# A third chunk of the dense layers beside the last rounds of an attention kernel

## The chip, the core and the metric

The kernel runs on one core of a Trainium2 chip. The core has five engines that run side by side, each with its own list of instructions in a fixed order: TensorE (PE, matrix products; PEld is its loading of weights), VectorE (DVE), ScalarE (ACT), GpSimd (POOL) and SyncE (SP, which here issues all transfers between memory and the core). An instruction waits until semaphores say that its inputs are there and its output's place is free; everything behind it on its engine waits with it. The metric is the time of one execution in microseconds (us) on the device, as the median of several runs.

## The reference

Three layers follow each other. x has 4 batches of 768 tokens and 512 columns.

```
attention: per head (8 heads, width 64) and per chunk of 32 tokens: softmax over 8 memory keys
           and the keys from 16 before to 8 behind the chunk, times the values
moe:       4 experts of width 64: causal softmax attention over 768 tokens, output wo[e],
           weighted by the gate (the best 2 of 4 experts for each token)
mixer:     h = transpose(x) @ U @ V          (U 768 x 32, V 32 x 768: mixes tokens)
           u = x + transpose(h)
           out = u + relu(u @ w_ch1) @ w_ch2 (w_ch1 512 x 2048, w_ch2 2048 x 512)
```

Below, "the attention" is all up to u, and "the dense layers" are the last line.

## The kernel before

Every product is made of three in a reduced precision (high part times high part, low times high, high times low), so each matrix is split into a high part (a copy on ACT) and a low part (a subtraction on DVE).

**The dense layers by chunks of tokens.** The 3072 tokens are taken in NCH = 6 chunks of 512. u is not formed: the kernel keeps z, which has 256 columns (the experts' outputs before wo, mixed), and multiplies w_ch1 by wo beforehand (`fuse_w1`, for four blocks j of 512 of the 2048 hidden columns; weights `wp_h`, `wp_l`). The 2048 hidden columns are 16 blocks f of 128. They are done in two parts:

- *Blocks f = 0 to 3 (FA = 4)*, in the plain way. For each chunk c, `load_z` loads z and splits it (`zh` on ACT, `zl` on DVE); `gemm1` makes one block of hidden columns: six matmuls `ph` (L285) of 512 columns, then `hh` (ACT, L293) and `hl` (DVE, L294); `gemm2` multiplies it by w_ch2: 3 matmuls `po` (L301) for each f and each of 4 output blocks m; `save_part` copies each finished `po` to `o` and stores it (L306, L308, L309). A chunk is 24 `ph` and 48 `po`, 72 matmuls of 512 columns in all.
- *Blocks f = 4 to 15* and the residual, by the scheme with seven products of half blocks (`right`, `multiply`, matmuls `acc`, L934). `right` makes the hidden block `t` (ACT, L866), sums of its quarters `sx` (DVE, L873), and splits them to `xhi` (ACT, L876) and `xlo` (DVE, L877). This is the last stage; it takes the chunks 0 to 5 again, one after the other.

**Three stretches.** (1) The attention, in rounds; the last batch (b = 3) has 12. Beside its rounds 0 to 5 block j = 0 of `fuse_w1` and the w_ch2 weights of the first part are prepared, and then `early` does the first part for the chunks below NEC. `early` is a generator: `fill` and `take` write its steps between and behind the rounds; each engine's order is then made when the program is built, by the readiness of steps and with the attention's steps ahead of `early`'s. (2) When the attention's pools are closed, `late` does the first part for the chunks NEC to 5; a second generator, `bg`, runs beside it and prepares the weights of the last stage: `fuse_w1` for j = 1, 2, 3 (matmuls `w1p`, L249) and `load_pair` for the pairs of blocks 8, 10, 16, 12, 14. The weights come as 64-bit numbers, and `decode` turns each block of 256 columns into 32 bit: a transfer `raw` (L122), one ACT step (L126), and three steps on DVE (L127, L128, L129); the split follows (L134 and L135, or L190 to L193). These transfers go to a pool that takes the place of the attention's buffers, so the first one waits until the attention's last result has been stored: that is `z` (DVE, L657, from matmuls `pz`, L656), stored as `zs` (L658). (3) The last stage. Its buffers (`hp`) are opened after `bg` has made its pairs up to 10 (`ready`).

```python
        late = list(range(NEC, NCH))
...
                if nxt is None and f == FS:
                    while not ready():
                        next(bg)
                    pass_a.close()
                    hp = p2.enter_context(tc.tile_pool(name="hp", bufs=1, side="right"))
...
                    for _ in range(BGA if nxt else 2 * BGA):
                        if not ready():
                            next(bg)
```

Of the kernel before, what the change touches and what calls it, by code (L numbers as in the profile page):

```python
# [52 lines left out]
VMP = 2  # L53
MS = 2
FA = 4
NEC = 2
BGA = 3
ND0, NW0, ND1, NW1 = 2, 2, 6, 3
LATE = 12
# [33 lines left out]
def tile_chunk_attention__moe_attention__mixer(  # L93
# [169 lines left out]
    def load_z(c):  # L263
        zf = (zp if wp2 is None else ea).tile([128, 2, CT], F32, name="zf", bufs=NZF)
        o = 0
        while o < CT:
            b, t = divmod(c * CT + o, S)
            n = min(CT - o, S - t)
            nc.sync.dma_start(zf[:, :, o:o + n], zs[b][:, :, t:t + n])
            o += n  # L270
        zh = zp.tile([128, 2, CT], F32R, name="zh", bufs=NZ)
        zl = zf.bitcast(F32R) if wp2 is None else zp.tile([128, 2, CT], F32R, name="zl", tag="zf", bufs=NZ)
        nc.scalar.copy(zh, zf)  # L273
        nc.vector.tensor_sub(zl, zf, f32(zh))
        zhl[c] = zh, zl
        zfs[c] = zf
# [34 lines left out]
    def early(ps):  # L311

        for c in range(NEC):
            load_z(c)
# [516 lines left out]
    with ExitStack() as p2:  # L831
# [49 lines left out]

        late = list(range(NEC, NCH))
        load_z(late[0])
# [170 lines left out]
```

## Time and profile before

| | us |
|---|---|
| median of 3 runs | 863.04 |
| the 3 runs | 862.87, 863.04, 864.9 |
| the profiled execution | 859.0 |
| its span, from the first to the last instruction | 857.2 |
| PE busy in the span | 811.0 |
| DVE busy in the span | 630.5 |
| ACT busy in the span | 494.8 |

In the profiled execution the attention's last product `pz` stands at 450.35 us, the first `acc` matmul of the last stage at 536.87 us. Between them lies the second stretch. Matmuls are pipelined: one of 512 columns is shown as about 0.39 us long, but the next one starts about 0.23 us after it. A busy share of PE is therefore no measure of how much of its time it used.

### The profile page before, as it was taken

How to read it: one execution, taken by the hardware profiler on the slowest of the kernel's cores; microseconds unless marked ns; L12 is line 12 of the kernel's file. 1: busy time of each engine (PE TensorE's matmuls, PEld its weight loads, DVE VectorE, ACT ScalarE, POOL GpSimd, SP SyncE). 2: the span in 40 equal slices, each digit the busy share in tenths (PEclk: the TensorE clock that was granted, in tenths of full speed). 3: DMA queues.
4: the chain of work that ended last, by engine and by line, in shares of the span. 5: the costliest groups of instructions: out<-in, count | busy, mean ns of one | idle time of the engine just before them, and what ended most of it. 6: DMA issues, size and time to landing. Idle time of an engine off the chain costs nothing.

```text
span 857.2 us, 18057 instructions
## 1 busy us (share of the span) xinstructions
PE 811.0 (95%) x6404; PEld 727.1 (85%) x6404; DVE 630.5 (74%) x1997; ACT 494.8 (58%) x1464; POOL 168.0 (20%) x254
## 2 busy tenths in 40 slices
PE   7889999999999998889979999999999999999995
PEld 5778999889987897768767878999989989899995
DVE  5687766577767766899536899989578495775947
ACT  3587766577656755656434566656464454645533
POOL 5334343344433424222110000000000000000002
PEclk8799999999999999999999999999999999999999
DMA  9644422133222201253206744301203012030101
GB/s 246 181 122 112 111 76 75 57 98 107 50 68 76 85 1 45 86 182 108 74 19 200 226 159 148 99 25 50 75 1 123 1 50 75 1 124 1 62 38 50
DMA packets 59627, 74.74 MB, mean 87 GB/s; under 512 B 29456, under 2 KB 34064, under 8 KB 58768
## 3 DMA queue, kind: packets, MB, share of 16 engines
q1 hardware_dynamic: 59536, 73.57, 27.9%
q8 instruction: 51, 0.84, 0.4%
q14 instruction: 40, 0.33, 0.1%
HBM read 57.83 MB, written 15.73 MB: 86 GB/s over the span
## 4 chain that ended last, share of the span: by engine, by line
PE 72%; DVE 9%; DMA 8%; ACT 6%; issue 3%; SPq 1%; POOL 1%; DVEq 0%; ACTq 0%; POOLq 0%
PE acc L934 23%; PE ph L285 14%; PE t L665 7%; PE pqk L468 5%; DMA raw<-in_w 4%; PE pv L508 3%; PE s L417 3%; PE tpc L600 3%; PE po L301 3%; PE sc L548 3%; PE sc L549 2%; PE tp L437 2%; DMA part<-o 2%; ACT a L424 1%; ACT ac L560 1%
## 5 line engine op out<-in xcount | busy, mean ns | idle before, releaser
L934 PE MATMUL acc<-xhi,sw 128*128 128x256 f32 x1008 | 191.6, 283 | 0.9 <-ACT xhi L876 0.9
L934 PEld LDWEIGHTS acc<-xhi,sw 128*128 128x128 f32 x1008 | 160.6, 189 | 8.1 <-ACT xhi L876 2.2
L934 PE MATMUL acc<-xlo,sw 128*128 128x256 f32 x504 | 139.2, 283 | 0.0
L873 DVE TENSOR_TENSOR sx<-t 128x256 f32<-128x256 f32 x180 | 67.8, 420 | 72.0 <-ACT t L866 72.0
L866 ACT ACTIVATE t<-ph 128x512 f32<-128x512 f32 x72 | 43.0, 597 | 121.2 <-PE ph L285 121.2
L582 POOL TENSOR_SCALAR ac<-ac,su,g 128x128 f32<-128x128 f32 (+5 forms) x96 | 70.0, 738 | 157.7 <-DVE su L580 102.7
L934 PEld LDWEIGHTS acc<-xlo,sw 128*128 128x128 f32 x504 | 95.4, 189 | 2.6
L925 POOL TENSOR_TENSOR pt<-pt,cp 128x512 f32<-128x512 f32 x3 | 6.4, 2155 | 408.6 <-DVE xlo L877 408.6
L876 ACT CAST xhi<-sx 128x256 fp32r<-128x256 f32 x210 | 76.0, 407 | 13.8 <-PE acc L934 6.2
L424 ACT ACTIVATE a<-a,nm 128x96 f32<-128x96 f32 x192 | 69.9, 367 | 22.9 <-DVE nm L421 22.2
L877 DVE TENSOR_TENSOR xlo<-sx,xhi 128x256 fp32r<-128x256 f32 x210 | 80.1, 421 | 3.8 <-ACT xhi L876 3.3
L560 ACT ACTIVATE ac<-sc,nmc 128x128 f32<-128x128 f32 (+5 forms) x96 | 60.4, 632 | 35.3 <-DVE nmc L575 20.3
L285 PE MATMUL ph<-zh,wp_l 128*128 128x512 f32 x192 | 61.0, 398 | 1.0 <-ACT zh L273 1.0
L417 PE MATMUL s<-k_t,qbd 128*128 128x96 f32 x384 | 56.3, 284 | 5.3 <-DMA k_t<-in_kw 4.0
L600 PE MATMUL tpc<-ident_s,ac 128*128 128x128 f32 x336 | 54.0, 279 | 7.0 <-ACT ath L603 2.9
L285 PE MATMUL ph<-zh,wp_h 128*128 128x512 f32 x192 | 60.3, 394 | 0.0
L429 POOL TENSOR_TENSOR a<-a,rs 128x288 f32<-128x288 f32 x64 | 42.6, 668 | 82.1 <-DVE rs L428 23.2
L417 PEld LDWEIGHTS s<-k_t,qbd 128*128 128x128 f32 x384 | 51.2, 200 | 8.1 <-issue 4.0
L285 PE MATMUL ph<-zl,wp_h 128*128 128x512 f32 x176 | 56.6, 393 | 0.0
L548 PE MATMUL sc<-kl,qs 128*128 128x384 f32 (+2 forms) x144 | 51.3, 357 | 2.6 <-DVE z L657 1.4
L421 DVE CUSTOM_DVE_ANT_0 a<-s,band_s 128x96 f32<-128x96 f32 x192 | 40.2, 252 | 16.6 <-PE s L417 13.9
L600 PEld LDWEIGHTS tpc<-ident_s,ac 128*128 128x128 f32 x336 | 39.5, 143 | 13.0 <-issue 6.2
(174 smaller groups left out, 2038.7 us busy)
## 6 DMA issues: line engine op xcount, KB each, us to landing
raw<-in_w SPq DMA_DIRECT2D x64, 256.0 KB, 3.5
k_t<-in_kw SPq DMA_DIRECT2D x32, 288.0 KB, 3.4
v_t<-in_vw SPq DMA_DIRECT2D x32, 288.0 KB, 3.2
qbd<-in_qT SPq DMA_DIRECT2D x64, 96.0 KB, 2.8
part<-o SPq DMA_DIRECT2D x24, 256.0 KB, 2.5
pt<-part SPq DMA_DIRECT2D x6, 1024.0 KB, 4.9
out<-pt SPq DMA_DIRECT2D x24, 256.0 KB, 2.5
zf<-zs SPq DMA_DIRECT2D x8, 512.0 KB, 4.7
```

Source lines behind the costliest of these rows:

```text
L285: nc.tensor.matmul(p, w[f // 4][:, pr, fs], z[:, pr], start=(n == 0), stop=(n == 5))
L417: nc.tensor.matmul(s[:, j, :], w["q"][:, qd * 3 + j], w["k"][:, qd * 3 + j], start=True, stop=True)
L424: nc.scalar.activation(a[:, j, :], a[:, j, :], AF.Exp, bias=nm[:, j:j + 1], scale=-1.0, accum_out=ss[:, j:j + 1])
L548: nc.tensor.matmul(s[:, o:o + w], q, kl[b, e, hf][:, :w], start=True, stop=False)
L560: nc.scalar.activation(aa[h][:, :n], src, AF.Exp, bias=nm[:, h:h + 1], scale=1.0, accum_out=su[:, h:h + 1])
L582: nc.gpsimd.tensor_scalar(aa[h][:, :n], aa[h][:, :n], su[:, h:h + 1], gates[b, i // 3][:, i % 3, 2 * pr + h:2 * pr + h + 1], op0=ALU.mult, ...
L600: nc.tensor.transpose(tp[h][:, j * 128:(j + 1) * 128], aa[h][:, j * 128:(j + 1) * 128], ident_s)
L665: session.append(nc.tensor.matmul(*a, **kw).ins)
L873: nc.vector.tensor_tensor(x, t[:, p[0], p[1]], t[:, q[0], q[1]], op=op)
L876: nc.scalar.copy(hi, x)
L877: nc.vector.tensor_sub(lo, x, f32(hi))
L934: nc.tensor.matmul(acc[n][:, m], w[:, ms], x, start=(f == FA and u == 0 and m == 0), stop=(f == NF - 2 and u == 2 and m == 1))
```

## The change

The number of chunks that `early` takes goes from two to three. The number that `late` takes falls from four to three. No operation is added or removed.

```diff
-NEC = 2
+NEC = 3
```

What each engine is given when the program is built changes as follows. First PE, at the end of the attention (`sc`: scores, `tpc`: transposes of the scaled exponentials `ac`, `t`: their product with the values, `pyt`: transposes for the mixer). Before, from a round's scores on:

```order
L549 MATMUL sc<-kd,qs 128x256
L551 LDWEIGHTS identb_s
L551 MATMUL sc<-tri_s,identb_s 128x128
L600 MATMUL tpc<-ident_s,ac 128x128 x8
L628 MATMUL pyt<-ident_s,yT 128x128 x6
L665 MATMUL t<-ath,vt 64x128 x8
```

Now, at the same place:

```order
L600 MATMUL tpc<-ident_s,ac 128x128 x4
L285 MATMUL ph<-zh,wp_l_5577 128x512 x2
L285 MATMUL ph<-zf,wp_h_5576 128x512 x2
L285 MATMUL ph<-zh,wp_h_5576 128x512 x2
L301 MATMUL po<-hh,w2l_5599 128x512
L285 MATMUL ph<-zh,wp_l_5577 128x512 x2
L285 MATMUL ph<-zf,wp_h_5576 128x512 x2
L285 MATMUL ph<-zh,wp_h_5576 128x512 x2
L301 MATMUL po<-hl,w2h_5598 128x512
L301 MATMUL po<-hh,w2h_5598 128x512
L600 MATMUL tpc<-ident_s,ac 128x128 x4
L628 MATMUL pyt<-ident_s,yT 128x128 x6
```

The third early chunk's `ph` and `po` stand between the transposes: 15 matmuls here, then 21 behind `pyt`, 18 behind the next round's scores, 6 between the two halves of the following transposes and 12 behind them, of which the last six are the first `ph` of the first late chunk. In all 72 more matmuls of 512 columns stand ahead of the last `pz` than before; from there to the first `acc` there are 72 fewer.

Second, DVE, from the attention's last `z` on. Before:

```order
L294 SCALAR_TENSOR_TENSOR hl<-ph,hh 128x512
L657 TENSOR_TENSOR z<-pz,yT 128x768
L274 TENSOR_TENSOR zl<-zf,zh 128x1024
L127 TENSOR_SCALAR d_t<-d_t 128x256
L128 SCALAR_TENSOR_TENSOR d_t<-raw_6567,d_t 128x256
```

Now:

```order
L294 SCALAR_TENSOR_TENSOR hl<-ph,hh 128x512
L657 TENSOR_TENSOR z<-pz,yT 128x768
L127 TENSOR_SCALAR d_t<-d_t 128x256
L128 SCALAR_TENSOR_TENSOR d_t<-raw_6680,d_t 128x256
L127 TENSOR_SCALAR d_t<-d_t 128x256
```

In both the decoding of `bg`'s weights follows at once. From the first of these L127 up to the first `xlo` of the last stage DVE has 184 instructions before and 187 now. Of the kinds, four `hl` fewer, and one L127, one L128, one L190 and four `sx` more; all others are as many as before.

Third, DVE at the start of the last stage. Before:

```order
L193 TENSOR_TENSOR swrh<-sw_7608,swrh 128x256
L193 TENSOR_TENSOR swrh<-sw_7612,swrh 128x256
L127 TENSOR_SCALAR hd_7906<-hd_7906 128x256
L873 TENSOR_TENSOR sx<-t 128x256
L190 TENSOR_TENSOR sw_7620<-hd_7601 128x256
L877 TENSOR_TENSOR xlo<-t,xhi 128x256
```

Now:

```order
L127 TENSOR_SCALAR hd_7905<-hd_7905 128x256
L873 TENSOR_TENSOR sx<-t 128x256
L190 TENSOR_TENSOR sw_7619<-hd_7600 128x256
L190 TENSOR_TENSOR sw_7623<-hd_7600 128x256
L873 TENSOR_TENSOR sx<-t 128x256 x4
L128 SCALAR_TENSOR_TENSOR hd_7905<-raw_7918,hd_7905 128x256
L127 TENSOR_SCALAR hd_7905<-hd_7905 128x256
L877 TENSOR_TENSOR xlo<-t,xhi 128x256
```

Four sums `sx` come ahead of the first `xlo`. On SP the order around the attention's last store stays: the last `zs` store, then six `raw` loads; the four stores of the third chunk's result now stand ahead of the `zs` stores.

## Rows read from the trace of the kernel before

**Rows 1.** Windows: us, busy PE, PEld, DVE, ACT, POOL; clock, DMA share, GB/s.
```profile
422.52:450.35 27.83, 21.94 (x187) 17.22 (x186) 11.15 (x22) 9.76 (x22) 3.67 (x4) 0.94 0.06 24
450.35:460.15 9.80, 8.81 (x38) 7.10 (x39) 2.69 (x3) 1.96 (x3) 0.00 (x0) 1.00 0.42 131
460.15:534.38 74.23, 72.31 (x382) 61.37 (x381) 68.14 (x187) 44.37 (x107) 0.00 (x0) 1.00 0.59 194
534.38:600.00 65.62, 65.62 (x456) 61.08 (x455) 61.95 (x172) 41.33 (x110) 0.00 (x0) 1.00 0.17 57
```

**Rows 2.** Timeline of PE at the attention's end: start, duration, [idle before <-releaser].
```profile
422.52 1.53 PE L665 MATMUL t<-ath,vt 128*64 128x128 f32 x24
...
426.13 0.63 PE L600 MATMUL tpc<-ident_s,ac 128*128 128x128 f32 x4 [0.77 <-ACT ath L603]
426.82 0.87 PE L628 MATMUL pyt<-ident_s,yT 128*128 128x128 f32 x6
...
431.93 1.62 PE L600 MATMUL tpc<-ident_s,ac 128*128 128x128 f32 x10 [1.40 <-ACT ac L560]
434.56 1.31 PE L665 MATMUL t<-ath,vt 128*64 128x128 f32 x20 [1.01 <-DVE ath L603]
...
438.22 0.59 PE L656 MATMUL pz<-v_st,qm 96*128 96x384 f32 x2 [1.57 <-DVE qm L648]
438.65 0.82 PE L600 MATMUL tpc<-ident_s,ac 128*128 128x128 f32 x6
440.02 1.33 PE L600 MATMUL tpc<-ident_s,ac 128*128 128x128 f32 x6 [0.55 <-DVE z L657]
441.15 1.27 PE L628 MATMUL pyt<-ident_s,yT 128*128 128x128 f32 x5
442.41 2.12 PE L665 MATMUL t<-ath,vt 128*64 128x128 f32 x24
444.89 0.33 PE L628 MATMUL pyt<-ident_s,yT 128*128 128x128 f32 x1 [0.37 <-ACT yT L618]
...
450.35 0.62 PE L656 MATMUL pz<-v_st,qm 96*128 96x384 f32 x2
```

**Rows 3.** The same timeline; 35 more matmuls of 512 columns stand between these two.
```profile
452.98 0.39 PE L301 MATMUL po<-hh,w2l 128*128 128x512 f32 x1
...
461.16 0.62 PE L285 MATMUL ph<-zl,wp_h 128*128 128x512 f32 x2
```

**Rows 4.** Windows as in rows 1, around the fall of the clock.
```profile
430.00:440.00 10.00, 5.34 (x54) 3.98 (x53) 4.47 (x9) 3.71 (x9) 1.94 (x2) 1.00 0.01 2
440.00:444.00 4.00, 3.98 (x29) 3.62 (x31) 0.96 (x1) 0.36 (x1) 0.00 (x0) 0.57 0.25 98
```

**Rows 5.** The chain that ended last, in order of time: start, us, what.
```profile
451.61 0.96 DVE z L657
...
452.58 4.29 DMA zs<-z
...
457.87 4.60 DMA raw<-in_w
```

**Rows 6.** Timeline of DVE: the first decoding step and the first `xlo`.
```profile
460.15 0.29 DVE L127 TENSOR_SCALAR d_t<-d_t 128x256 uint32<-128x256 uint32 x1 [6.46 <-ACT d_t L126]
...
534.38 0.42 DVE L877 TENSOR_TENSOR xlo<-t,xhi 128x256 fp32r<-128x256 f32 x1
```

**Rows 7.** Timeline of PE: the first matmuls of the last stage.
```profile
536.87 0.40 PE L934 MATMUL acc<-xhi,sw 128*128 128x256 f32 x2
```

**Rows 8.** Waits of DVE from 460.15 to 534.4: total us, times, longest.
```profile
DVE d_t L127 <- ACT d_t L126: 8.2, 4, 6.5
DVE o L308 <- DMA part<-o: 2.8, 2, 2.2
```

**Rows 9.** DVE's work in that stretch by line: busy us, mean ns of one.
```profile
L294 DVE SCALAR_TENSOR_TENSOR hl<-ph,hh 128x512 fp32r<-128x512 f32 x12 | 8.2, 684 | 0.3 <-ACT hh L293 0.3
...
L873 DVE TENSOR_TENSOR sx<-t 128x256 f32<-128x256 f32 x1 | 0.4, 419 | 0.0
```

## The prediction

> **What bounds the kernel now.** I read the busy time by windows first, since the whole span hides that the stretches have different limits. In the last stage PE is busy without a gap, 65.62 of 65.62 us from 534.38 on [rows 1]; nothing there changes, so whatever moves the first `acc` moves the end by the same amount. The question is when that first matmul, now at 536.87 [rows 7], can start. Two stretches lie before it.
>
> At the attention's end, from 422.52 to the last `pz` at 450.35, PE is busy 21.94 of 27.83 us [rows 1]. The timeline shows why: short products that wait for each other's copies. The reader is to see the idle times in brackets, 0.77, 1.40, 1.01, 1.57, 0.55 and 0.37, together 5.67 us [rows 2], which a product that depends on none of this could fill. There is a second loss. The granted clock is 1.00 up to 440 and 0.57 from 440 to 444, that is mostly the lower level of 1.2 GHz, after ten microseconds in which PE was busy for 5.34 [rows 4]. The same 24 `t` matmuls take 1.53 us at 422.52 and 2.12 at 442.41 [rows 2].
>
> Between `pz` and `acc` PE seems full too, 72.31 of 74.23 us. But DVE is busy 68.14 of the same 74.23 [rows 1], nearly all of it `bg`'s weights. So two engines are close to full in this stretch, and the change takes work from only one of them.
>
> **The change, term by term**, against the profiled execution's 859.0 us.
>
> *1. Seventy-two matmuls come ahead of `pz`.* From 452.98 to 461.16 36 matmuls start, one every 0.227 us [rows 3]. 72 x 0.227 = **+16.4 us** on PE's list before the attention's last product. The list is in order, so an attention matmul that is ready stands behind them.
>
> *2. The idle time that they fill.* They stand behind the first half of the `tpc` at 425, behind the scores before 431.93, and around the `tpc` before 434.56. That covers the waits of 0.77, 1.40 and 1.01 us, **-3.2 us**. The groups there are 15, 18 and 12 matmuls, 3.4, 4.1 and 2.7 us, longer than the waits, so the rest is pure delay; the 21 behind `pyt` stand where PE did not wait at all. The waits of 1.57, 0.55 and 0.37 lie in the last chain of `pz`, `tpc` and `pyt`, where no new matmul is put. Bounds: nothing is filled (if ACT and DVE, which get the chunk's copies too, answer later by as much), or all 5.67.
>
> *3. The clock.* If PE is kept busy from 430 to 440, the clock should not fall. At full clock the 24 `t` would take 1.53 for 2.12, the six `tpc` 0.82 for 1.33, the five `pyt` about 0.8 for 1.27 (from six at 0.87) [rows 2]: 0.6 + 0.5 + 0.5 = **-1.6 us**. Bounds 0 and -1.6. The Trainium skill, TensorE: Matmul & The Clock Gate (Part 1), says that the array's clock is halved by default and that activity releases it; by that, too, the 1.6 us are given back, and [rows 4] agree as far as they show a fall behind a thinly used stretch.
>
> So the last `pz` moves by 16.4 - 3.2 - 1.6 = **+11.6 us**, to about 462 (bounds +9.1 and +16.4).
>
> *4. From `pz` to the decoding.* `z` is made at 451.61, its store takes 4.29 us to land, the first `raw` loads follow [rows 5], and DVE, idle for 6.46 us, starts decoding at 460.15 [rows 6]. The loads need the place of the attention's buffers, so they can't start sooner: these 9.80 us [rows 1] stay behind `pz` and move with it. The third chunk's four stores stand ahead of `zs` on SP, but its last `po` stand ahead of the last but one `pz` already, so I cost them at nothing; were they late, a store's landing, 4.29 us in [rows 5], would be about what they add.
>
> *5. DVE's work up to the first `xlo`.* Its list has four `hl` fewer, at 0.684 us [rows 9] 2.7 us; and more: one L127 at 0.29 [rows 6], one L128, one L190 and four `sx`, all of 128x256, at 0.419 like the `sx` in [rows 9], 0.29 + 6 x 0.419 = 2.8 us. The sum is **0.0**: DVE still has 68.1 us of work [rows 1]. The other side is PE: its 86.5 us from `pz` to `acc` fall by 16.4 to 70.1, while DVE's way is 9.8 + 68.1 = 77.9 without a single gap. PE arrives early and waits; what was taken from it is not gained.
>
> *6. DVE's gaps.* Of the 74.23 us it was idle 6.1. The largest causes are the landing of the first loads (8.2, of which 6.46 are those ahead of 460.15) and `o`'s two buffers, 2.8, waiting for stores [rows 8]. Both loads and stores keep their pattern; four fewer `hl` mean a little less waiting on ACT. I take **-1.0 us**, with -6.1 (no gap left) and +4 (one more wait for a store's landing of some 4 us) as bounds.
>
> *7. From the first `xlo` to `acc`.* Now 2.5 us pass (534.38 to 536.87) because PE comes later than DVE. With PE waiting instead, the first `acc` can follow at once: **-2.2 us**, bounds 0 and -2.5. Afterwards DVE, 61.95 of 65.62 us busy from there to 600 [rows 1], has as much to do as before, and the sums that four `sx` made early are missing later; I cost this at nothing. If PE's head start is spent waiting for `xlo` instead, this term is 0.
>
> Sum: 11.6 + 0.0 - 1.0 - 2.2 = **+8.4 us**, 867.4 against 859.0. The profiled execution stands 4.0 us below the median of the runs, 863.04; with that the forecast is **871.4 us**, slower by 1.0%. All bounds together give +0.5 (9.1 - 6.1 - 2.5) and +20.4 (16.4 + 4).
>
> **The rivals.**
>
> *PE stays the bound, and the change gains.* Then the 72 matmuls are only moved, and the filled waits and the clock are the result: -3.2 - 1.6 = -4.8, or 858.2 us. For it: PE's 72.31 of 74.23 busy [rows 1], and the idle brackets [rows 2], which are real. It decides only if DVE gets from `pz` to `acc` in about 70 us; term 5 gives 77.9 as the least. But a busy share of PE counts overlapping matmuls (0.39 us each, one every 0.227), while DVE's counts work. The Trainium skill, Perfetto Trace Analysis (Optimization Strategy), says that where the busiest engine changes over time, interleaving such regimes may improve a kernel; that is this rival, and the rows show the interleaving on PE but not on DVE, whose work stays where it was. Chance 6%.
>
> *Everything falls well: no change.* All idle time is filled, DVE loses nearly all gaps, `acc` follows at once: +0.5 to +2.6, 863.5 to 865.6 us. For it: gaps on DVE do shrink when PE runs ahead. Against it: most have their cause in transfers. Chance 13%.
>
> *Nothing is absorbed.* ACT and DVE get 4 `hh`, 4 `hl`, a split of z and four copies more in the attention's end, in order, between the steps that the chain waits for; if each wait only moves, terms 2 and 3 fall away (+4.8), and if the clock falls while PE waits in the second stretch, and is low where `acc` begins, some 2 us more are lost, as from 440 to 444: about 878 us. For it: PE will wait there some 12 us in all. Against it: DVE is busy 11.15 of 27.83 us at the attention's end [rows 1]. Chance 12%.
>
> *The chunk is not put where the change means it.* The new order shows it between the rounds, so this is out.
>
> **How the numbers follow.** 69% for the forecast, 6%, 13% and 12% for the others. Its own bounds reach from about +4 to +13 (term 2 or 3 missing, or gaps half gone). The range leaves out the gain and the best of the no-change cases below, and the far end of the last rival above: 865.0 to 878.0. A difference of 0.3%, 2.6 us, is about what a measurement of this kernel can tell from none: 6% faster, 13% within, 81% slower.
>
> **What would show it.** Right: the last `pz` 10 to 13 us later, with the waits before `tpc` and `t` gone and no fall of the clock there; the first decoding step about 10 us behind `pz`; DVE's busy time between that and the first `xlo` again near 68 us; and new waits of PE in that stretch, some 10 us, on `w_l` and `w_h` of `fuse_w1` and on `xhi` or `xlo`, where before there were 2 us. Wrong: a `pz` that moves by under 8 us; or a DVE that starts or ends this work sooner, above all loads that begin before the last `zs` store has landed; or a first `acc` less than 80 us behind `pz`.

## The result, and the profile after

The changed kernel takes 872.2 us (median of 4 runs, 870.62 to 874.0), the kernel before 863.17 us on the same chip. The ratio is 1.0101 with a 95% interval of 1.0077 to 1.0125: slower by 1.0%, +9.0 us, where +8.4 us was forecast.

The profiled execution of the changed kernel has a span of 870.7 us and a time of 872.46 us, about its median; that of the kernel before was 4.0 us below its own. So the two traces differ by 13.5 us, 4.5 more than the medians. Part of it can be seen: the `t` of 24 at the head of the attention's end starts at 424.71 in place of 422.52 [rows 2], 2.2 us before any of the 72 matmuls in question. The rest is therefore read in steps from that row on.

The first view is the table of windows of the changed kernel (us, then busy time of PE, PEld, DVE, ACT, POOL; granted clock, DMA share, GB/s), cut at the same events as [rows 1].

```profile
424.71:463.75 39.04, 36.04 (x259) 28.95 (x258) 16.43 (x29) 14.08 (x29) 3.69 (x4) 1.00 0.15 53
463.75:471.59 7.84, 6.19 (x20) 4.75 (x21) 1.56 (x3) 1.03 (x2) 0.00 (x0) 0.78 0.38 128
471.59:548.22 76.63, 65.37 (x339) 55.71 (x338) 68.44 (x190) 45.04 (x111) 0.00 (x0) 0.93 0.59 188
548.22:614.00 65.78, 65.48 (x450) 61.05 (x449) 59.14 (x166) 38.59 (x100) 0.00 (x0) 0.98 0.13 41
```

In the first line stand 259 matmuls where there were 187, and the stretch is 39.04 us long in place of 27.83. In the third PE is busy 6.9 us less than before, but DVE has 68.44 us of work for 68.14, and the stretch did not become shorter: 76.63 for 74.23. That is the change in two lines: 11 us are paid ahead of `pz`, and almost nothing comes back behind it.

| Step | before | after | difference | forecast |
|---|---|---|---|---|
| `t` at the attention's end to the last `pz` | 27.83 | 39.04 | +11.2 | +11.6 |
| last `pz` to the first decoding step of DVE | 9.80 | 7.84 | -2.0 | 0 |
| first decoding to the first `xlo` | 74.23 | 76.63 | +2.4 | -1.0 |
| first `xlo` to the first `acc` | 2.49 | -0.15 | -2.6 | -2.2 |
| first `acc` to the end of the span | 320.33 | 322.63 | +2.3 | 0 |
| sum | | | +11.3 | +8.4 |

The sum is 2.3 us more than the medians differ by. Which step is too long in these two executions cannot be told from them.

The timeline of PE at the attention's end in the changed kernel answers to [rows 2].

```profile
452.68 0.59 PE L656 MATMUL pz<-v_st,qm 96*128 96x384 f32 x2 [1.57 <-DVE qm L648]
453.11 0.82 PE L600 MATMUL tpc<-ident_s,ac 128*128 128x128 f32 x6
454.49 0.85 PE L600 MATMUL tpc<-ident_s,ac 128*128 128x128 f32 x6 [0.55 <-DVE z L657]
455.17 0.71 PE L628 MATMUL pyt<-ident_s,yT 128*128 128x128 f32 x5
456.38 1.53 PE L665 MATMUL t<-ath,vt 128*64 128x128 f32 x24 [0.51 <-DVE ath L603]
458.28 0.33 PE L628 MATMUL pyt<-ident_s,yT 128*128 128x128 f32 x1 [0.37 <-ACT yT L618]
...
463.75 0.44 PE L656 MATMUL pz<-v_st,qm 96*128 96x384 f32 x1
```

The waits of 1.57, 0.55 and 0.37 us are still there, as they were forecast to be; those of 0.77, 1.40 and 1.01 are gone from this stretch, and one of 0.51 is new. The second `tpc` takes 0.85 us where it took 1.33, the 24 `t` 1.53 where they took 2.12 [rows 2].

The windows of the changed kernel show the granted clock, first at the place of [rows 4], then where the last stage begins.

```profile
430.00:440.00 10.00, 10.00 (x64) 8.13 (x63) 5.02 (x8) 3.03 (x6) 1.27 (x2) 1.00 0.11 28
440.00:444.00 4.00, 4.00 (x20) 3.27 (x20) 1.67 (x4) 2.32 (x5) 1.58 (x2) 1.00 0.35 131
...
540.00:544.00 4.00, 0.00 (x0) 0.00 (x0) 4.00 (x13) 2.07 (x6) 0.00 (x0) 0.65 0.41 123
544.00:548.00 4.00, 2.65 (x6) 2.17 (x7) 3.94 (x13) 3.62 (x11) 0.00 (x0) 0.50 0.88 284
548.00:552.00 4.00, 4.00 (x18) 3.65 (x17) 4.00 (x14) 1.76 (x5) 0.00 (x0) 0.57 0.07 31
```

At the attention's end the fall of the clock is gone: 1.00, where [rows 4] had 0.57, and 1.00 for the whole way up to `pz`, where [rows 1] had 0.94. It has moved to another place. PE did nothing from 540 to 544, and the clock that it was granted there fell to 0.50, the level of 1.2 GHz, and stayed low until behind 550, when the last stage had begun. Why PE did nothing is in its waits (total us, times, longest) from 440 to 570 us:

```profile
PE ph L285 <- ACT t L866: 8.1, 1, 8.1
PE po L301 <- ACT hh L293: 2.7, 1, 2.7
```

and in its timeline just ahead of the last stage:

```profile
536.94 0.28 PE L249 MATMUL w1p<-w_h,wt_h 128*128 128x256 f32 x1
545.35 1.22 PE L285 MATMUL ph<-zh,wp_l 128*128 128x512 f32 x2 [8.13 <-ACT t L866]
...
548.07 1.70 PE L934 MATMUL acc<-xhi,sw 128*128 128x256 f32 x7
```

PE is through with the dense layers and with `fuse_w1` at 537 and then waits 8.13 us in one piece. The `t` that it waits for (ACT, L866) is the first step that writes into the pool `hp`. In ACT's list it stands behind steps of `bg` that waited for loads, as the chain that ended last shows (start, us, what):

```profile
537.25 3.92 DMA hd<-in_wo
541.20 0.58 ACT swrl L192 x2
541.78 2.58 DMA raw<-in_w
544.38 0.44 ACT hd L126
544.81 0.49 ACT t L866
```

DVE's list comes to the same place at the same time. The window shows DVE without a gap, and the timeline gives the two ends of its list, to be read against [rows 6], and the first `sx` made of this `t`:

```profile
521.59:541.59 20.00, 15.20 (x88) 13.03 (x86) 19.99 (x55) 11.76 (x30) 0.00 (x0) 0.99 0.29 97
```

```profile
471.59 0.29 DVE L127 TENSOR_SCALAR d_t<-d_t 128x256 uint32<-128x256 uint32 x1 [5.63 <-ACT d_t L126]
...
545.33 0.42 DVE L873 TENSOR_TENSOR sx<-t 128x256 f32<-128x256 f32 x1
...
548.22 0.42 DVE L877 TENSOR_TENSOR xlo<-t,xhi 128x256 fp32r<-128x256 f32 x1
```

DVE takes this `sx` without a wait, straight from `bg`'s steps. Had the loads come sooner, `t` might have been made sooner, but DVE would still have been at `bg`'s weights. How much that would have given is not shown.

### The profile page after: what moved, and what is told of

It is laid out like the page before. It is cut to its first block, busy times and chain, and to the rows that moved or that the text cites. A ratio compares the mean times of both kernels' runs of the same rounds, so it can differ in the third digit from the quotient of the medians.

```text
span 870.7 us, 18055 instructions
## 1 busy us (share of the span) xinstructions
PE 813.8 (93%) x6404; PEld 731.2 (84%) x6404; DVE 632.3 (73%) x1997; ACT 497.0 (57%) x1464; POOL 167.9 (19%) x254
## 4 chain that ended last, share of the span: by engine, by line
PE 77%; DVE 7%; DMA 7%; ACT 5%; issue 2%; SPq 1%; POOL 1%; DVEq 0%; ACTq 0%; POOLq 0%
PE acc L934 23%; PE ph L285 15%; PE t L665 7%; PE po L301 6%; PE pqk L468 5%; PE pv L508 3%; PE tpc L600 3%; PE s L417 3%; DMA raw<-in_w 3%; PE sc L548 3%; PE sc L549 2%; PE tp L437 2%; PE w1p L249 1%; DMA part<-o 1%; ACT a L424 1%
## 5 line engine op out<-in xcount | busy, mean ns | idle before, releaser
L866 ACT ACTIVATE t<-ph 128x512 f32<-128x512 f32 x72 | 43.0, 599 | 124.3 <-PE ph L285 124.2
L876 ACT CAST xhi<-sx 128x256 fp32r<-128x256 f32 x210 | 76.2, 408 | 16.4 <-DVE sx L873 9.5
L285 PE MATMUL ph<-zl,wp_h 128*128 128x512 f32 x168 | 54.2, 397 | 0.0
L421 DVE CUSTOM_DVE_ANT_0 a<-s,band_s 128x96 f32<-128x96 f32 x192 | 40.1, 252 | 17.0 <-PE s L417 13.6
L665 PE MATMUL t<-ath,vt 128*64 128x128 f32 x672 | 47.0, 280 | 3.0 <-DVE ath L603 2.6
```

The lines of the kernel that those rows point to most:

```text
L285: nc.tensor.matmul(p, w[f // 4][:, pr, fs], z[:, pr], start=(n == 0), stop=(n == 5))
L665: session.append(nc.tensor.matmul(*a, **kw).ins)
L876: nc.scalar.copy(hi, x)
```

## The experiments

Each kernel was timed against the kernel before on the same chip; ratios are to that kernel, with 95% intervals. Its medians there were 861.16, 861.38 and 861.6 us in the three groups of four kernels. The changed kernel was not timed again beside them, so a kernel is compared with it by two ratios, most with an interval of 0.2 to 0.4% to either side: a difference of less than some 3 us cannot be told. "Ahead" is the number of `ph` and `po` matmuls ahead of the last `pz`: 168 in the kernel before, 240 in the changed one. The table collects what the traces show (one execution each); the text takes them in order.

| Kernel | ahead | ratio | first `ph` to last `pz` | last `pz` to `acc` | DVE busy, decoding to `xlo` | `acc` to end |
|---|---|---|---|---|---|---|
| before | 168 | 1 | 78.84 | 86.52 | 68.14 | 320.33 |
| changed | 240 | 1.0101 | 91.50 | 84.32 | 68.44 | 322.63 |
| e1_held | 174 | 0.9975 | 79.88 | 83.37 | 67.21 | 320.56 |
| e12_held_again | 174 | 0.9990 | 84.09 | 83.74 | 67.35 | 321.68 |
| e2_four | 288 | 1.0223 | 101.54 | 82.54 | 67.50 | 322.30 |
| e5_one_chunk | 96 | 1.0091 | 69.16 | 104.32 | 76.20 | 320.57 |
| e11_third_po_held | 217 | 1.0101 | 91.58 | 80.31 | 67.43 | 321.03 |
| e3_light_three | 240 | 1.0048 | 90.39 | 73.94 | 54.82 | 323.46 |
| e4_light_two | 168 | 1.0034 | 80.95 | 88.03 | 60.88 | 320.75 |
| e6_three_gpsimd | 240 | 1.0110 | 93.10 | 79.68 | 63.48 | 326.27 |
| e7_two_thirds_gpsimd | 217 | 1.0121 | 93.97 | 83.67 | 68.47 | 321.37 |
| e9_three_act_copies | 240 | 1.0100 | 94.02 | 81.66 | 63.61 | 320.34 |
| e10_held_act_copies | 174 | 0.9982 | 79.93 | 85.52 | 65.37 | 320.76 |
| e8_three_warm | 240 | 1.0083 | 90.93 | 83.11 | 68.23 | 321.81 |

How far one execution can be trusted is seen in e1_held and e12_held_again, which are the same kernel: 4.2 us apart up to `pz`, 0.4 from there to `acc`, 1.1 behind it. The 4.2 us go with the granted clock. The windows from the first `ph` to the last `pz`, of e1_held and of e12_held_again:

```profile
370.89:450.77 79.88, 71.41 (x482) 57.79 (x482) 55.70 (x127) 41.33 (x99) 15.09 (x16) 1.00 0.28 93
```

```profile
372.69:456.78 84.09, 75.83 (x483) 61.54 (x482) 55.47 (x127) 41.09 (x99) 14.78 (x16) 0.94 0.26 89
```

So the fall of the clock in the attention's last rounds, which term 3 counts on, comes in one execution of a kernel and not in another. In the seven traces with 168 to 217 matmuls ahead it fell in the last 40 us before `pz` in five (not in e1_held and e10_held_act_copies); in the six with 240 or more it was 1.00 there each time.

### Where the third chunk stands: e1_held

```diff
-NEC = 2
+NEC = 3
...
             for f in range(FA):
-                gemm1(ps, c, f, TL)
+                with tc.issue_after(hold[HAT]) if c == 2 else ExitStack():
+                    gemm1(ps, c, f, TL)
```

> Three early chunks as in the change, but the hidden blocks of the third one may only be issued after the attention's last transposes. In the order that this gives, 174 matmuls of the first part stand ahead of the last pz, against 168 before and 240 with the change. Theory (the loss is the delay of pz, since DVE's work behind it is not shortened): about as before, 862 to 866 us. Rival (the third early chunk costs by itself, through its buffers, its stores on SP or the missing fourth late chunk): about as with the change, 870 to 873 us.

Measured: 859.09 us, 0.9975 (0.9953 to 0.9998), some 3 us below the theory's range and far from the rival's. The chunk is still taken by `early`, but its products come behind the attention, and the loss is gone. So it lies in the place of its products, with the copies that follow them, and not in its buffers or in the loading of its z.

### How many: e2_four and e5_one_chunk

```diff
-NEC = 2
+NEC = 4     (e5_one_chunk: NEC = 1)
```

> Four early chunks. 288 matmuls of the first part stand ahead of the last pz, 48 more than with the change, 10.9 us at 0.227 us. Theory: no idle time of PE is left to fill there and DVE's work from the last z to the first xlo stays as it is (one us more by its list), so nearly all of it is lost: 880 to 885 us. Rival (PE's total work sets the time and the 9 us of the change are waits that arose once at the switch): 871 to 875 us.

> Early part of one chunk of 512 tokens (two in the kernel before), nothing else changed. Theory (the second stretch ends when the later of PE and DVE is through; with fewer early chunks it is PE): 72 matmuls x 0.227 = 16.4 us go from ahead of the last pz to behind it; ahead, waits of 3 to 5 us that they filled come back, so the last pz comes 11 to 13 us sooner; pz to acc grows by 14 to 17 us, to 100 to 104, all of it PE's (PE busy in over 95% of it). Sum +2 to +5 us: 863 to 867, ratio 1.002 to 1.006. Rival (DVE's list sets the second stretch whatever the number of chunks): the list grows by about 7 us, pz to acc about 94, and the sum is -4 to -6: 855 to 858.

Four chunks: 879.9 us, 1.0223 (1.0169 to 1.0277), at the edge of the theory's range. One chunk: 868.75 us, 1.0091 (1.0061 to 1.0121), slower than both expectations. The windows from the last `pz` to the first `acc`, first of e2_four, then of the kernel with one chunk:

```profile
474.86:557.40 82.54, 59.45 (x309) 50.66 (x309) 69.75 (x197) 44.55 (x112) 0.00 (x0) 0.85 0.54 171
```

```profile
440.51:544.83 104.32, 100.28 (x500) 83.89 (x501) 82.22 (x213) 55.07 (x126) 0.00 (x0) 1.00 0.54 174
```

With one chunk PE is busy 96% of the stretch and sets its length, as the theory had it. With four PE is busy 72% of it, and the stretch is 82.54 us all the same; its largest wait is again the one for `t`, 12.6 us; a second, of 8.0, is for `zh`. From 174 to 288 matmuls ahead the stretch stays at 80 to 84 us in the seven kernels of the table whose DVE has 67 to 69 us to do. That is a floor that PE's work does not reach through, and the reason why the third chunk is not paid back. One chunk lost more than was expected, 1.0091 for 1.002 to 1.006: the last `pz` came 9.7 us sooner and not 11 to 13, and the stretch behind it grew by 17.8 and not 14 to 17. From the first `ph` to `pz` PE was idle for 11.5 us where it had been 6.9, which is within the 3 to 5 us that were expected to come back. The clock there was 0.94 for 0.98; whether that is the rest was not tried.

### What makes the floor: e3_light_three and e4_light_two

Both leave out the sign step of the decoding (L128) in the second stretch, so that DVE has less to do; the weights made there lose their sign.

```diff
-        nc.vector.scalar_tensor_tensor(t, h, 0x80000000, t, op0=ALU.bitwise_and, op1=ALU.bitwise_or)
+        if nd[0] != ND1:
+            nc.vector.scalar_tensor_tensor(t, h, 0x80000000, t, op0=ALU.bitwise_and, op1=ALU.bitwise_or)
```

> Three early chunks, and the decoding of the weights in the second stretch leaves out its sign step (L128), so that the signs of these weights are lost. By the list DVE's work from the last z to the first xlo falls by 14 us. Theory (DVE sets this stretch once PE is relieved): pz does not move, the first acc comes 11 to 14 us sooner, until PE's own 70 us set it; the clock's fall at its start goes too: 858 to 862 us. Rival (the loss lies in the attention's end alone, and DVE only follows): 869 to 872 us.

> Two early chunks as before, with the same sign step left out in the second stretch; DVE's work there falls by 8.5 us by the list. Theory (with two early chunks PE sets this stretch, with some 2 to 3 us of idle time): 860 to 863 us, so that three early chunks are then as fast or faster than two, by up to the 4.8 us of filled waits and clock. Rival (DVE sets it with two chunks as well): 854 to 856 us.

Three chunks with less work on DVE: 864.9 us, 1.0048 (1.0029 to 1.0066). Two chunks with less: 863.04 us, 1.0034 (1.001 to 1.0057). The windows from the last `pz` to the first `acc`, of e3_light_three and of e4_light_two:

```profile
460.90:534.84 73.94, 68.65 (x357) 57.88 (x357) 54.45 (x144) 41.03 (x100) 0.00 (x0) 0.98 0.59 187
```

```profile
453.32:541.35 88.03, 84.21 (x428) 70.01 (x429) 66.30 (x173) 49.11 (x118) 0.00 (x0) 1.00 0.58 186
```

The same step left out is worth 10.4 us of this stretch with three chunks (84.32 to 73.94) and nothing with two (86.52 to 88.03). So DVE's list holds the stretch with three, and PE's holds it with two: with one chunk more behind `pz` the stretch grew by 17.8 us, and with 7.3 us less on DVE it did not shrink (1.0034 is even a little above the kernel before). That is what the prediction said of both. That three would then be as fast as two or faster was not seen: 1.0048 and 1.0034 do not differ by more than their intervals. In time the relief gave back about half of the 1.0%, less than the trace's 10.4 us, and 864.9 lies between the theory's range and the rival's; the profiled execution of e3_light_three, 860.11 us, was its fastest, 4.8 below its median. Against the kernel before, its trace has 11.6 us more up to `pz`, 12.6 less from there to `acc` and 3.1 more behind it, where the clock is low again (0.59 in the first 4 us behind `acc`).

### Relieving DVE with the whole computation kept: e6, e7, e9, e10

In e6_three_gpsimd and e7_two_thirds_gpsimd GpSimd makes the low part of each split in the second stretch; e7 also holds the third chunk's second products until the attention is through, as e11 below. In e9 (three chunks) and e10 (as e1_held) ACT makes all copies of finished sums there.

```diff
-        nc.vector.tensor_sub(lo, v, f32(hi))
+        (nc.gpsimd if nd[0] == ND1 else nc.vector).tensor_sub(lo, v, f32(hi))
```

```diff
-        if m % 2:
+        if m % 2 or nd[0] == ND1:
             nc.scalar.copy(o, po)
```

> Three early chunks, and in the second stretch the low part of each weight's split (L135, 24 subtractions up to the first xlo) is made by GpSimd in place of DVE; the computation is complete. Theory (with three chunks DVE's work is the second stretch's bound): DVE's busy time between the first decoding and the first xlo falls from 68.4 to 55 to 60 us, pz to acc from 84.3 to 74 to 78 us, ratio to the kernel before 1.002 to 1.006 in place of 1.010. Rival (transfers or the chain of ACT and DVE per weight set the pace, not DVE's sum): pz to acc stays at 82 to 85 and the ratio at 1.008 to 1.012; GpSimd slower than DVE in this would look the same, and show as DVE and ACT waiting for GpSimd.

> GpSimd as in the run before, and of the third chunk only the first products (ph) run beside the attention, its second products (po) only after the attention is through: 217 early matmuls ahead of the last pz in place of 240 (168 in the kernel before). Complete computation. Theory (the best balance is where PE and DVE get through the second stretch together): last pz +6 to +8 us, pz to acc 74 to 78 us, that is -8 to -12, sum -1 to -5: ratio 0.994 to 0.999. Rival (every matmul ahead of pz costs its full 0.227 us, and what GpSimd takes over comes back as waits): ratio 1.002 to 1.006.

> Three early chunks, and in the second stretch every copy of a finished partial sum out of the accumulator (o, 128x512, 0.69 us each) is made by ACT instead of every other one by DVE; complete computation. Seven of DVE's copies up to the first xlo go, 4.5 us by the rows, with the 3.2 us that DVE waited there for stores. ACT has 45 of 76.6 us busy in that stretch, so it has room. Theory (DVE's list bounds the second stretch with three chunks, and GpSimd did not help only because DVE's own steps became longer beside it): DVE's busy time between first decoding and first xlo falls from 68.4 to 63 to 65 us, pz to acc from 84.3 to 77 to 81 us, ratio to the kernel before 1.003 to 1.007 in place of 1.010. Rival (not DVE's sum but the chain of loads, ACT and DVE per weight sets the pace): pz to acc 83 to 85, ratio 1.008 to 1.012.

> The third chunk's first products held until the attention is through (as e1_held: 174 early matmuls ahead of the last pz), and all copies of partial sums by ACT in the second stretch. Theory (here PE and DVE need about the same time in the second stretch, so that relief of DVE alone gives no more than its gaps): ratio 0.994 to 0.999. Rival (DVE alone still sets the end there): pz to acc falls by 4 us to 79 or less, ratio 0.990 to 0.994.

Measured: e6 872.04 us, 1.011 (1.0071 to 1.0149); e7 872.14 us, 1.0121 (1.0083 to 1.016); e9 869.91 us, 1.01 (1.0074 to 1.0125); e10 860.04 us, 0.9982 (0.9963 to 1.0002). For e6 and e9 the theory's ratio was missed and the rival's came, while the stretch, 79.68 and 81.66 us, fell short of the rival's 82 and 83: a part of the relief came. e7 was slower than theory and rival both. For e6 a reason is in the trace. These lines give the durations of e6's steps in the second stretch (ns, shortest, median, longest), first GpSimd's, then DVE's:

```profile
L135 POOL TENSOR_TENSOR w_l<-d_t,w_h x24: 722/765/5709, 475.2 to 534.8; 128x256 fp32r<-128x256 f32 x24
...
L127 DVE TENSOR_SCALAR d_t<-d_t x24: 277/282/825, 472.3 to 520.3; 128x256 uint32<-128x256 uint32 x24
L128 DVE SCALAR_TENSOR_TENSOR d_t<-raw,d_t x24: 408/413/977, 472.6 to 521.6; 128x256 uint32<-128x256 uint32 x24
```

DVE's steps, which never took longer than 0.30 and 0.43 us in the changed kernel, take up to 0.83 and 0.98 beside GpSimd, and one of GpSimd's took 5.7. The timelines of both engines suggest that each is held up while the other works. POOL's four from 525.39 on:

```profile
525.39 8.69 POOL L135 TENSOR_TENSOR w_l<-d_t,w_h 128x256 fp32r<-128x256 f32 x4 [6.42 <-ACT w_h L134]
534.76 0.73 POOL L135 TENSOR_TENSOR w_l<-d_t,w_h 128x256 fp32r<-128x256 f32 x1 [0.69 <-ACT w_h L134]
```

and DVE's in that time:

```profile
525.41 0.28 DVE L127 TENSOR_SCALAR hd<-hd 128x256 uint32<-128x256 uint32 x1
...
531.71 0.41 DVE L190 TENSOR_TENSOR sw<-hd 128x256 f32<-128x256 f32 x1
535.02 0.75 DVE L193 TENSOR_TENSOR sw<-hd,sw 128x256 fp32r<-128x256 f32 x1 [2.91 <-ACT sw L192]
```

While DVE runs without a gap from 525.41 to 532.1, GpSimd finishes one of the four, the one of 5.7 us, and two of the other three fall into the time when DVE sits idle; the DVE step at 535.02, beside GpSimd's at 534.76, takes 0.75 in place of 0.41. The Trainium skill, SBUF — State Buffer (Who interferes with whom), says that DVE and GpSimd have one pair of ports in common and that the loser of the two blocks fully, also where DVE only reads two inputs from SBUF; these rows agree, in that both engines' steps became longer, but that the ports are the cause they do not show. So 24 x 0.42 = 10.1 us taken off DVE gave 5.0 (68.44 to 63.48), and the last stage had 4.9 us of waits behind its first `acc`, where the changed kernel has 1.2.

In e9 nothing of that kind happened, DVE's busy time fell as expected to 63.61 us, and still little was won: 81.66 us from `pz` to `acc`. DVE's waits in e9, from its first decoding step's wait on:

```profile
DVE d_t L127 <- ACT d_t L126: 9.0, 3, 5.7
DVE w_l L135 <- ACT w_h L134: 5.9, 5, 2.9
```

In the changed kernel the same two lines were 6.8 and 2.0 us. So of 4.8 us less work on DVE 2.7 came out of the stretch, and the rest turned into waits, above all for ACT. ACT's `d_t` waited for the loads of `raw` (11.0 us in e9, 9.6 in the changed kernel, 6.8 of them at the start in both), and its `w_h` for PE, whose `w1p` had not yet used the last one (4.2 and 5.4 us). "DVE's sum sets the stretch" is too simple, then. DVE's list is full without a gap only in its last 27 us or so (from 521.59 to 541.59 it is busy 19.99 of 20.00 in the changed kernel). Before that it depends on loads, on ACT and on PE: from 491.59 to 531.59 PE is busy all 40.00 us and DVE 35.17. What one takes off DVE there can become idle time. e3 took 13.6 us off DVE, from the weights at the end of the list too, and got 10.4 of them. What e10 shows fits: where PE's and DVE's lists are about equally long, relieving one of them changes nothing, 0.9982 beside e1_held's 0.9975 and e12's 0.999.

### The filled waits: e11_third_po_held, and e12

```diff
-NEC = 2
+NEC = 3
...
-                    gemm2(po, c, f, m, f == FA - 1, f == 0)
+                    with tc.issue_after(hold[HAT]) if c == 2 and m >= 0 else ExitStack():
+                        gemm2(po, c, f, m, f == FA - 1, f == 0)
```

> Of the third chunk the first products (ph) run beside the attention, its second products (po) are held until the attention is through: 217 early matmuls ahead of the last pz, between the 174 of e1_held and the 240 of the changed kernel; DVE as in the changed kernel. Theory (beyond about 174 every matmul put ahead costs its 0.227 us less what it fills, and gives nothing back, since DVE sets the second stretch): last pz 6 to 8 us later than before, pz to acc 83 to 86, ratio 1.004 to 1.009. Rival (the second stretch gets shorter with PE's work until 240): pz to acc 78 to 80, ratio 0.997 to 1.001.

> e1_held once more, with more rounds and beside the others: 174 early matmuls ahead of the last pz. Theory (about as many ahead as before, a few more in gaps): ratio 0.995 to 1.000, so at or just below the kernel before. Rival (the lower time of e1_held was scatter of the start): 0.999 to 1.003.

e11: 869.83 us, 1.0101 (1.008 to 1.0122), above the ranges of both expectations and as slow as the changed kernel, with 23 matmuls fewer ahead of `pz`. From `pz` to `acc` it took 80.31 us, near the rival's 78 to 80 and not the theory's 83 to 86, so a little does come back behind `pz`. What was lost lies ahead of it. The 23 matmuls are worth 23 x 0.227 = 5.2 us, yet from the first `ph` to the last `pz` it took 91.58 us as against 91.50. PE's timeline and the windows of e11 say why:

```profile
448.06 0.98 PE L657 MATMUL pz<-v_st,qm 96*128 96x384 f32 x2 [1.57 <-DVE qm L649]
448.84 2.93 PE L601 MATMUL tpc<-ident_s,ac 128*128 128x128 f32 x12
```

```profile
440.00:444.00 4.00, 2.81 (x23) 2.42 (x25) 1.16 (x3) 1.47 (x3) 1.94 (x2) 0.72 0.13 41
444.00:448.00 4.00, 2.50 (x23) 1.59 (x19) 0.78 (x3) 0.71 (x3) 0.00 (x0) 0.50 0.00 0
448.00:452.00 4.00, 3.94 (x17) 3.57 (x18) 1.15 (x2) 0.80 (x1) 0.00 (x0) 0.50 0.25 98
```

Held back, the 48 `po` of the third chunk all came to stand between the last two `pz`, behind the round with the idle time (and put 23 `ph` of the next chunk behind the last `pz`). That round is about as thinly used as in the kernel before, and its clock falls to 0.50, as it fell to 0.57 there; the twelve `tpc` take 2.93 us, where the changed kernel needs 0.82 and 0.85 for them. So it counts where the matmuls stand, and 5 us is about the 4.8 that the prediction gave the filled waits and the clock. It is no measure of these two terms: it is one execution, the clock stays low longer than in the kernel before, and the clock alone made 4.2 us between e1_held and e12_held_again.

e12: 860.12 us, 0.999 (0.9968 to 1.0011), which both expectations allow. With e1_held and e10 there are three timings of a third chunk held back, all slightly below 1, two of them with intervals that include it. A version that clearly beats the kernel before was not found.

### The clock where the last stage begins: e8_three_warm

Twenty-four matmuls of 128x512, whose result nobody uses, are put into PE's list between the last `w1p` and the `ph` that waits for `t`.

```diff
+        wz = zhl[0][0]
+        wtile = ps.tile([128, CT], F32, name="pwarm2", **TF)
+        for _ in range(24):
+            nc.tensor.matmul(wtile, wp_h[1][:, 0, :128], wz[:, 0], start=True, stop=True)
```

> Three early chunks, and 24 matmuls of 128x512 whose result nobody uses (added work) between the last w1p and the ph that waits 8.1 us for ACT's t, ahead of the last stage. Theory (the 2.3 us that the last stage is longer after the change are the low clock in which it begins, 0.50 from 540 to 550 us, behind that wait): the granted clock stays at 1.00 where the first acc run, acc to the end is 320.0 to 321.0 us in place of 322.6, pz to acc unchanged at 83 to 86, ratio 1.007 to 1.009. Rival (the last stage is longer because sums of the third chunk that were made early are missing in it, or by work of DVE): acc to the end stays at 322 to 323.5 though the clock is 1.00.

869.13 us, 1.0083 (1.005 to 1.0115). The windows of ten us from the first `acc` on, of the changed kernel and then of e8_three_warm:

```profile
548.07:558.07 10.00, 10.00 (x62) 9.46 (x61) 10.00 (x32) 6.46 (x20) 0.00 (x0) 0.83 0.19 63
```

```profile
544.69:554.69 10.00, 9.89 (x68) 8.97 (x67) 10.00 (x32) 6.93 (x20) 0.00 (x0) 1.00 0.22 75
```

The clock is 1.00 where it was 0.83, and PE gets 68 matmuls done in place of 62. From `acc` to the end it is 321.81 us, between the theory's 320 to 321 and the rival's 322 to 323.5. The first row alone puts the clock's share at an estimated 0.17 x 10 = 1.7 us of the 2.3. Two other kernels agree: e9 has three chunks like the changed one and e11 holds the third chunk's `po` back; the clock was 0.97 and 0.99 in their first ten us, and their last stages took 320.34 and 321.03. That all of the 2.3 is the clock is not shown: traces with 1.00 there reach from 320.3 to 321.8 us, and the ratio's interval includes the changed kernel's 1.0101.

## Why the prediction was right

**Terms 1 to 3, right.** 72 matmuls came ahead of `pz`, and 16.4 us of them became 11.2, where 11.6 was forecast. The waits of 0.77, 1.40 and 1.01 and the fall of the clock are gone as the prediction named them. That the two are worth 4.8 us together is not measured apart, and the clock's part hangs on the execution of the kernel before that was profiled: e1_held and e12_held_again show that such a fall may come or stay away.

**Term 4, mis-sized.** The prediction kept the 9.80 us from `pz` to the decoding; they became 7.84. In the queue of SP the first `raw` load follows once the store `zs` has landed. The changed kernel's queue and its chain of waits:

```profile
465.99 0.32 SPq L658 DMA_DIRECT2D zs<-z  x1
468.42 2.71 SPq L122 DMA_DIRECT2D raw<-in_w  x6
471.17 0.52 SPq L269 DMA_DIRECT2D zf<-zs  x1
```

```profile
465.99 2.30 DMA zs<-z
...
469.28 4.41 DMA raw<-in_w
```

The store landed in 2.30 us, not in the 4.29 of [rows 5], and DVE began 2.0 us sooner behind `pz`, which the prediction had listed as a sign of being wrong. This is hardly scatter: the two profiled kernels with two chunks in their usual place (the kernel before and e4) show 4.3 and 4.0 us, the twelve others 2.3 to 2.5. Why is open (last section).

**Term 5, right in its number.** DVE's busy time is 68.44 us for the 68.1 forecast, and PE came early and waited, 8.1 and 2.7 us. The place of the wait was not foreseen: the prediction looked for it on `w_l`, `w_h`, `xhi` or `xlo`, and it is one wait for ACT's `t`, behind two loads of `bg`'s weights in ACT's list; DVE's list, full up to that point, ends there too.

**Term 6, wrong in sign.** The gaps of DVE were to shrink by 1.0 us; they grew from 6.1 to 8.2. With term 4 the sum is +0.4 for the way from `pz` to the first `xlo`, for -1.0 forecast. The reason given, less waiting on ACT, is what failed: DVE's `w_l` waited 2.0 us for ACT's `w_h`, and before not at all, and ACT's `w_h` waited 5.4 us for PE's `w1p`, where before it was 0.4. DVE's `hl` waited 1.3 us for ACT's `hh`, before 0.3.

**Term 7, right, and given back.** `acc` follows the first `xlo` at once, -2.6 us for -2.2. But PE had stood still before it, and the clock was low where the last stage begins: +2.3 us. This is the piece that the third rival named, "is low where `acc` begins, some 2 us more are lost", and it belonged into the forecast, since the forecast itself said that PE would wait some 10 us.

**How much was luck.** The main mechanism came as forecast: the delay of `pz` is paid, and DVE's list keeps the stretch from getting shorter. That the median came within 0.6 us of +8.4 is in part luck. Terms 4 and 6 and the last stage were each off by 2.0 to 3.4 us, one down and two up, and the traces' own sum is +11.3.

The rivals: that PE stays the bound is out (DVE's list holds the stretch with three chunks: e3, e4); that all falls well ended at 865.6 us and is out by over 6; that nothing is absorbed is out, since the waits and the fall of the clock went away; its piece on the clock came.

## What to carry to other kernels

Work that is moved ahead of another stage is paid back only if its engine holds the stage that it is taken from; here the second engine of that stage was as full, so the second chunk ahead paid (without it the kernel is 0.9% slower), and the third did not. Read the busy time of every engine in the stretch, and not only of the one whose work is moved; and where the sum says that an engine will wait, look where its clock will be when it goes on. Here, taking work off the full engine gave its full worth only where its list had no gaps already; elsewhere a part of it became waits.

## What the runs showed of the hardware

- Behind a stop of PE of 8.13 us the granted clock was 0.50 from 542 to 550 us, also while PE was busy without a gap from 545.35 on, and 1.00 again from 552 on. With 24 matmuls in that stop it was 1.00 at the first `acc`.
- Two executions of one kernel (e1_held and e12_held_again) had a mean granted clock of 1.00 and 0.94 over the same stretch, 79.88 and 84.09 us long, at the same work of PE.
- A subtraction of 128x256 on GpSimd took 0.72 us at its fastest and 5.7 at its slowest while DVE worked; DVE's steps of 0.28 and 0.41 us took up to 0.83 and 0.98 beside it.
- The store of `z`, 384 KB, landed in 4.3 and 4.0 us in the two kernels named under term 4. In both of these, and in none of the twelve others, the transfers of the 5 us behind it include one packet of the queue that loads instructions, of 0.02 MB. A `zf` load behind the store is no sufficient reason: in e1_held and e5_one_chunk it stands 1.13 us behind it too, and the store landed in 2.3. That the packet is the cause was not tried.
